# A new front for a long convolution: k without halo rows, a smaller second table, another order

## The chip, the cores and the metric

The kernel runs on one core of a Trainium2 chip. Its time is the device time of one launch in microseconds (us); lower is better. PE, DVE, ACT, POOL and SP are the engines' names in the profile (TensorE, VectorE, ScalarE, GpSimd, SyncE); SP only issues transfers here.

## The reference, cut to what matters

All inputs are bf16; S = 2048 rows, D = 512 channels.

```python
kv = shift(k, 4 taps per channel) * v
y  = causal_convolution(kv, ssm_k) + kv * ssm_D     # FFT of length 2S along S
h  = q + layernorm(q) * y
n  = layernorm(h)
g  = gelu(layernorm(n) @ w1)                          # 512 x 512
x1 = n + shifts_by_quarter(g) @ w2                    # 512 x 512
out = h + x1 + gelu(layernorm(x1) @ w3) @ w4          # 512 x 1792, 1792 x 512
```

## The kernel before, in words

The convolution is done as a Fourier transform in stages on PE. The work, in order:

- *Front.* `load_k`, `load_v`, `load_h` bring k, v and the filter in. `k_transposed` turns rows of k on PE into `kT` (in the slot `kta`). `k_taps` forms the four taps as matmuls of `kT` with `dg`, a row of diagonal matrices with the tap weights (L292), into `psh`; DVE multiplies with v into `kvq` (L404). `k_rows` moves `kvq` into the layout `Rk` by 16 transfers. `h_layout` does the same for the filter on PE (`pt`, evicted into `Rh`). Because rows of k are spread over partitions 16 by 16, the first three rows of a partition need the last rows of the one before it: these are loaded as separate halo rows, with a memset for partition 0 (L270).
- *Tables.* The cosines and sines are made on the chip: POOL writes integers (`iota`, L302), `phase` multiplies them and takes them modulo the circle (L306 on DVE or POOL, L309 on DVE), ACT takes the sine (`sine` L313, `cosine` L318 and L320). The first table is `WA`, the last one `Wf` and its second half `Wf2`. The second table `Wc` is a matrix with zeros except in every fourth column: POOL sets it to zero by 12 memsets (L334), the values are computed in `tta` over 2 x 1024 columns, and four transfers (L354) spread them into `Wc`.
- *First stage* (`stage_a`, L446): 16 tiles for k (`pak`) and 16 for the filter (`pah`), evicted into `Tk` and `Th`.
- *Second stage* (`stage_c`, L470 to L473): products with `Wc`, evicted into `xt`; `product` multiplies the two spectra on DVE (L586, L590, L593) into `Yp`. Between these DVE takes the statistics of q (L552, L553).
- *Back.* `pg` (L647) and its evictions `Gs`, then the last level `py` with `Wf`; `gate` (L711, L713) multiplies with the normalized q (`qn`, L632 and L635) and adds q.
- *MLP.* w1 and w3 by `gelu_mm` (L768), w2 (L828), w4 (L890), with transposes between.

Work is not issued in the order of the program text. Every step is recorded with the steps it depends on, and a list `ISSUE`, written out, gives the order in which all steps are issued and, for a step that two engines can do, the engine (A, V, G). Each engine takes its own steps in that order, and waits where a step is not ready; steps behind it wait too.

```python
for word in ISSUE.split():
    i = int(word.rstrip("AVG"))
    where, fn, deps = self.ops[i][:3]
```

Large buffers lie in named slots that are reused: "C" (k, v, Rk, later Yp), "S1" (filter, later q), "B" (kT, dg, later Tk), "A" (tables, later Th), "W" (Wc, later the weights).

Of the kernel before, what the change touches and what calls it, by code (L numbers as in the profile page):

```python
# [16 lines left out]
P = 128  # L17
S = 2048
# [8 lines left out]
EPS = 1e-5  # L27

# [12 lines left out]
25 3 0 5 7 4 1 2 49 9 26 8 11 29 24 21 6 50V 31 23 13 10 51 16 85 32G 14 22 52 12 20 86V 87 48 15 19 40 74 17 98  # L41
88A 27 34 46 108 35V 99A 37 75 91 109V 53 36 89 39 92 66 76G 28 102 67 90 33 97 100 93 103 62 18 128 30 94 57G
96 47 131 68 101 133 64 38 107 134 132V 104 42 69 105 95 44 63 106 65 77 118 78V 41 79 135V 110 80 54G 83 58 84
45 59 55 112 60 43 119V 129 70 113 71 73 72 111 136 130A 81 117 82 115 122 114 212 137A 120 123 56 61 200 121
138 210 179 201A 208 211V 186 126 209A 127 196 124 187V 197A 206 125 184 116 213 207A 185V 188 214 182 189A 183V
180 139 190 181A 204 202 140G 205V 191A 155 156A 203V 153 163 154A 147 164V 173 148A 174V 151 149 152A 167 141
169 150A 168V 171 170A 177 172V 159 178A 198 160V 175 199A 157 176V 158A 161 192 223 162A 165 239 257 166A 243
194 235 258 195A 261 224 241 193A 259 245 225 142 263 244 260V 265 262A 143 240 237 266A 273 219 144G 264A 275
221 217 277 274A 267 271 276A 289 238 268 272A 287 246 270 278A 283 215 290A 269 285 229 284A 297 280 288A 279
286A 295 236 282 298A 299 281 301 296A 233 313 291 302A 307 292 300A 309 230 294 314A 311 293 308A 242 304 310A  # L50
319 303 312A 321 222 306 325 320A 305 323 231 322A 315 326A 337 316 324A 331 234 317 338A 335 318 332A 333 218
327 345 336A 328 347 334A 343 227 346A 329 349 420 330 348A 385 363 366 226 340 365 344A 339 367 364 228 342
350A 341 145 352 146 351 220 354 353 232 396 216 355 247 356 394 397A 248 358 398 249 357 395A 250 360 359 399A
390 251 400 362 368 391A 252 361 392 253 401V 414 393A 406 254 407V 416 415A 404 417A 255 405V 410 402 411A 408
256 403V 388 409A 386 389V 387A 412 379V 421 413A 380V 371V 373V 370A 418 422 369V 382A 383V 374V 384V 430 378V
423A 372V 375V 381A 424 457 431A 425 428 376A 465 432 458A 426 433 466A 492 429 434 419 500 436 435 427 437 467
377A 438 493A 501A 527 459 441A 468 442A 460 443A 445 469 444A 463 535 446A 470 471 689 464 528A 461 447 472 462
494 448A 473 536A 455 502 477A 495 476A 503 479A 480 496 453 478A 537 481A 449 498 506 454 482 504 456 483A 507
499 451 497 505 538 450 508 486 452 488 487 490 541 512A 484 539 489 511V 491 529 515 485 474 568 530 516A 569
542 531 514A 513V 533 517 532 572 534 540 518A 439 475 543 521 525 440 546A 547V 509 570 522 550 510 571 526 523  # L60
551A 549V 519 548V 575 524 552 520 577 553A 573 595 578 574 579 556 581 554 557 580 576 582 583 558 555 560 559
592 596 585A 584V 561 597 587A 588 594 615 589A 586V 593 565 590 617 618 591A 600 601 544 616 714 562 716 566
715 567 564 692 545 717 563 598 696 693 599 604 690 605 602 698 647 699 697 691 704 649 708 619 705 603 712 606
709 706 713 702 707 607V 700 620 703 608 609V 710 701 648 610 694 711 623 650 627 695 624 613A 718 719 614 653
611V 621 612 625 622 626 628 629 630 651 631 652 659 657 734 658 660 728 671 632 655 735 633 736 654 723 729 738
634 635 672 724 673 674 675 676 636 637 638 645V 639A 643V 646 739 640 737 644 750 725 752 751 677 727 678 742
679 753 680 641V 720 730 642 743 726 748 731 656 722 661 662 732 663 721 685V 749 756 686 744 733 740 687V 745
761 688 754 741 664 746 665 755 666 667 668 788 669 747 670 681V 770 762 771 789 786 763 768 787 799 778 784 779
683V 769 684 757 682 785 764 765 824 758 780 825 759 794 772 781 760 782 773 766 783 774 767 792 775 790 793 776
791 818 777 826 819 804 827 806 805 828 807 820 829 830 821 812 831 800 813 814 801 808 815 822 809 810 816 811  # L70
823 795 817 833 796 832 798 802 803 797 838 834 837 836 835 842 839 841 840 843 844 845
# [3 lines left out]
class Plan:  # L75
# [7 lines left out]
    def __init__(self, rings):  # L83
        self.ops, self.last, self.rd = [], {}, {}
        self.rings, self.tiles = rings, {}

    def add(self, where, fn, r=(), w=(), opens=None, lat=None):
        i = len(self.ops)
        deps = set()
# [32 lines left out]
def kernel(  # L122
# [48 lines left out]
    slot("C", [P, 24064], "kin")  # L171
    slot("S1", [P, DC, S], "hraw")
    slot("B", [P, 11776], "kta")
    slot("A", [P, 16384], "tta")
    slot("W", [P, 3, 16, 4, N2, 4], "Wc")
    slot("S2", [P, N2, 2 * P], "Rh")

    def k_sb():
        return X["kin"][:, 0:9728].rearrange("p (r d) -> p r d", d=D)

    def v_sb():
        return X["kin"][:, 9728:15872].rearrange("p (b t d) -> p b t d", b=3, d=D)

    def Rk():
        return X["kin"][:, 15872:24064].rearrange("p (n d) -> p n d", d=2 * P)

    def kT():
        return X["kta"][:, 0:9728].rearrange("p (c r s) -> p c r s", c=DC, s=P)

    def dg():  # L190
        return X["kta"][:, 9728:11776].rearrange("p (c j s) -> p c j s", c=DC, s=P)

    def trc(a):
        return X["tta"][:, 2048 * a:2048 * a + 2048]

    def uu(i):
        return X["tta"][:, 6144 + 2048 * i:8192 + 2048 * i].bitcast(I32)

    def um():
        return X["tta"][:, 14336:14848].bitcast(I32)  # L200
# [4 lines left out]
    kd = A_k[0]  # L205
    vd = A_v[0].rearrange("(p t) d -> p t d", t=NT)

    def dma(us, fn, r=(), w=()):
        add({"S": us}, fn, r, w)

    def load_k(r0, r1):
        dma(1.4, lambda: nc.sync.dma_start(k_sb()[:, r0:r1, :], bass.AP(
            kd.tensor, kd.offset + (r0 - 3) * D, [[NT * D, P], [D, r1 - r0], [1, D]])),
            r=("C",), w=[("k", r) for r in range(r0, r1)])

    def load_v(qr):
        dma(1.4, lambda: nc.sync.dma_start(v_sb()[:, qr % 3, :, :], vd[:, 4 * qr:4 * qr + 4, :]),
            r=("C",), w=[("v", qr % 3)])

    def load_h(c):  # L220
        dma(1.4, lambda: nc.sync.dma_start(X["hraw"][:, c, :], A_ssm_k[c * P:(c + 1) * P, :]),
            r=("S1",), w=[("h", c)])

    dma(0.5, lambda: nc.sync.dma_start(ssk_bf[:], A_shift_k.rearrange("(c p) j -> p c j", p=P)), w=["sskb"])
    load_k(3, 7)
    for p0, p1 in ((NT, P), (1, NT)):
        dma(0.6, lambda p0=p0, p1=p1: nc.sync.dma_start(k_sb()[p0:p1, 0:3, :], bass.AP(
            kd.tensor, kd.offset + (NT * p0 - 3) * D, [[NT * D, p1 - p0], [D, 3], [1, D]])),
            r=("C",), w=[("kh", p0)])
    load_v(0)  # L230
    load_k(7, 11)
    load_v(1)
    load_k(11, 15)
    dma(0.5, lambda: nc.sync.dma_start(dcol[:], A_ssm_D.rearrange("(c p) -> p c", p=P)), w=["dcol"])
    load_h(0)
    load_h(2)
    load_k(15, 19)
    load_v(2)
    load_h(1)
    load_h(3)  # L240

# [3 lines left out]
    wlo = cst.tile([P, 1], F32)  # L245
    ident = cst.tile([P, P], BF16)
    pidx = cst.tile([P, 1], I32)
    i4 = cst.tile([P, 4], F32)
    pint = cst.tile([P, 6], I32)
# [6 lines left out]
    p64, n2T, k2X, d4X = (pf[:, i:i + 1] for i in (0, 1, 3, 4))  # L256
    k1F, offF = pf[:, 6:7], pf[:, 7:8]
# [4 lines left out]
    def small():  # L262
# [4 lines left out]
        V.memset(wlo[:], -4096.0)  # L267

    add({"V": 0.4}, small, w=["warm", "mpi"])
    add({"V": 0.7}, lambda: V.memset(k_sb()[0:1, 0:3, :], 0.0), r=("C",), w=[("kh", 0)])  # L270
# [9 lines left out]
    def numbers():  # L280
        V.tensor_scalar(pint[:, 0:1], pidx[:], 63, None, op0=OP.bitwise_and)
        V.tensor_scalar(pint[:, 1:2], pidx[:], 2, None, op0=OP.logical_shift_right)
        V.tensor_scalar(pint[:, 2:3], pidx[:], 3, None, op0=OP.bitwise_and)
        V.tensor_scalar(pint[:, 3:4], pidx[:], 31, None, op0=OP.bitwise_and)
        V.tensor_scalar(pint[:, 4:5], pidx[:], 5, None, op0=OP.logical_shift_right)
        V.tensor_scalar(pint[:, 5:6], pidx[:], 6, None, op0=OP.logical_shift_right)
        V.tensor_copy(pf[:, 0:6], pint[:])
# [645 lines left out]
```

## Time and profile before

| what | us |
|---|---|
| three runs | 263.15, 260.5, 263.21 |
| their median | 263.15 |
| span of the profiled execution | 260.4 |
| PE busy | 227.0 (87%) |
| DVE busy | 180.7 (69%) |
| ACT busy | 152.7 (59%) |
| POOL busy | 30.0 (12%) |
| share of DMA engines' time taken by the program's queue | 28.7% |

The profiled execution is told by its span alone, 260.4 us from its first to its last instruction; the lowest of the three times, 260.5, is 0.1 above it. In the first 60 us all engines share the work of the front; from 60 to 110 DVE is busy without a break; from about 127 on PE is. In lines of the timeline the first number is the start in us from the span's beginning, the second the length, and x16 that sixteen like it are drawn together; a bracket tells the idle time before it and what ended it.

### The profile page before, as it was taken

How to read it: one execution, taken by the hardware profiler on the slowest of the kernel's cores; microseconds unless marked ns; L12 is line 12 of the kernel's file. 1: busy time of each engine (PE TensorE's matmuls, PEld its weight loads, DVE VectorE, ACT ScalarE, POOL GpSimd, SP SyncE). 2: the span in 40 equal slices, each digit the busy share in tenths (PEclk: the TensorE clock that was granted, in tenths of full speed). 3: DMA queues.
4: the chain of work that ended last, by engine and by line, in shares of the span. 5: the costliest groups of instructions: out<-in, count | busy, mean ns of one | idle time of the engine just before them, and what ended most of it. 6: DMA issues, size and time to landing. Idle time of an engine off the chain costs nothing.

```text
span 260.4 us, 4761 instructions
## 1 busy us (share of the span) xinstructions
PE 227.0 (87%) x1933; PEld 148.4 (57%) x1946; DVE 180.7 (69%) x410; ACT 152.7 (59%) x194; POOL 30.0 (12%) x37
## 2 busy tenths in 40 slices
PE   2959998989987929657699999999999999999993
PEld 2859998869987918523345454444444444444441
DVE  8895849979999999999999964897290421001341
ACT  2618158997989969999887664524163307604000
POOL 8989200303000000000000000000000000000000
PEclk9986999797999988997799999999999999999999
DMA  6986494970000079200000000020450021000141
GB/s 186 359 320 202 130 256 126 199 149 3 3 1 3 0 269 381 81 0 0 0 3 0 1 0 4 20 60 0 63 123 19 20 63 40 0 0 3 26 95 41
DMA packets 25044, 21.15 MB, mean 81 GB/s; under 512 B 14655, under 2 KB 21823, under 8 KB 24894
## 3 DMA queue, kind: packets, MB, share of 16 engines
q1 hardware_dynamic: 25022, 20.85, 28.7%
q8 instruction: 15, 0.25, 0.4%
q14 instruction: 7, 0.06, 0.1%
HBM read 13.50 MB, written 2.10 MB: 60 GB/s over the span
## 4 chain that ended last, share of the span: by engine, by line
PE 49%; DVE 23%; issue 1%; ACT 1%
PE pw L768 24%; PE p L890 18%; DVE Yp L586 7%; PE p L828 5%; DVE bst L552 3%; DVE Gs L163 2%; DVE Yp L590 2%; DVE Yp L593 2%; PE pt L756 2%; DVE qn L635 1%; DVE wts L711 1%; DVE hh L713 1%; ACT hh L740 1%; DVE mvq L553 1%; DVE xt L163 0%
## 5 line engine op out<-in xcount | busy, mean ns | idle before, releaser
L768 PE MATMUL pw<-act,wts 128*128 128x512 bf16 x285 | 65.3, 383 | 1.5 <-ACT act L161 1.3
L772 ACT ACTIVATE g<-pw 128x512 bf16<-128x512 f32 x56 | 32.5, 596 | 48.9 <-PE pw L768 48.9
L890 PE MATMUL p<-wts,g 128*128 128x512 bf16 x217 | 48.8, 379 | 0.3
L768 PEld LDWEIGHTS <-wts 128*128 128x128 bf16 x288 | 28.4, 99 | 35.4 <-issue 3.1
L895 DVE TENSOR_TENSOR wts<-p,wts 128x1024 bf16<-128x1024 f32 (+1 forms) x9 | 9.9, 1106 | 54.2 <-PE p L890 48.4
L890 PEld LDWEIGHTS <-g 128*128 128x128 bf16 x224 | 21.9, 98 | 26.4
L399 PE MATMUL psh<-kta 128*128 128x128 bf16 x256 | 17.7, 239 | 3.1 <-ACT tta L313 3.1
L586 DVE TENSOR_TENSOR Yp<-xt 128x2048 bf16<-128x2048 bf16 (+1 forms) x20 | 19.3, 999 | 0.0
L399 PEld LDWEIGHTS <-kta 128*128 128x128 bf16 x256 | 17.2, 108 | 3.3 <-issue 3.3
L161 ACT CAST xt<-pch 128x1024 bf16<-128x1024 f32 x16 | 16.1, 1041 | 2.4 <-PE pch L473 1.5
L470 PE MATMUL pck<-Tk,Wc 128*128 128x256 bf16 x64 | 16.1, 290 | 1.6 <-ACT xt L161 1.3
L472 PEld LDWEIGHTS <-Wc 128*128 128x128 bf16 x128 | 14.8, 115 | 2.8 <-issue 2.8
L161 ACT CAST xt<-pck 128x1024 bf16<-128x1024 f32 x15 | 15.2, 1034 | 1.0 <-DVE Yp L586 1.0
L834 DVE SCALAR_TENSOR_TENSOR x<-hh,rho,p 128x512 bf16<-128x512 bf16 x16 | 11.7, 739 | 5.5 <-PE p L828 5.5
L470 PE MATMUL pch<-Th,Wc 128*128 128x256 bf16 x64 | 14.7, 272 | 0.9 <-ACT xt L161 0.7
L473 PEld LDWEIGHTS <-Wc 128*128 128x128 bf16 x128 | 14.8, 115 | 0.5
L828 PE MATMUL p<-wts,act 128*128 128x512 bf16 x61 | 14.8, 379 | 0.2
L404 DVE TENSOR_TENSOR kvq<-psh,kin 128x1024 bf16<-128x1024 f32 x8 | 9.7, 1220 | 7.6 <-PE psh L399 7.6
L470 PEld LDWEIGHTS <-Wc 128*128 128x128 bf16 x128 | 14.8, 115 | 0.1
L473 PE MATMUL pck<-Tk,Wc 128*128 128x128 bf16 x64 | 14.7, 229 | 0.0
L472 PE MATMUL pck<-Tk,Wc 128*128 128x128 bf16 x64 | 14.7, 229 | 0.0
L647 PE MATMUL pg<-CSG,Yp 128*128 128x128 bf16 x128 | 9.3, 236 | 5.8 <-DVE Yp L590 5.1
(130 smaller groups left out, 407.1 us busy)
## 6 DMA issues: line engine op xcount, KB each, us to landing
wts<-in_B_w_dram SPq DMA_DIRECT2D x2, 1792.0 KB, 10.1
kin<-in_A_k_dram SPq DMA_DIRECT2D x4, 512.0 KB, 7.1
kin<-in_A_v_dram SPq DMA_DIRECT2D x4, 512.0 KB, 6.9
hraw<-in_A_ssm_k_dram SPq DMA_DIRECT2D x4, 512.0 KB, 9.0
kin<-kvq SPq DMA_DIRECT2D x16, 128.0 KB, 3.3
q_sb<-in_A_q_dram SPq DMA_DIRECT2D x2, 1024.0 KB, 10.6
out_dram<-wts SPq DMA_DIRECT2D x14, 128.0 KB, 2.3
Wc<-tta SPq DMA_DIRECT2D x4, 384.0 KB, 5.6
```

The costliest lines, as they stand in the source:

```text
L161: A.copy(o, src)
L399: T_.matmul(pv[:, i, c * P:(c + 1) * P], lhsT=kT()[:, c, t0 + i + 3 - j, :], rhs=dg()[:, c, j, :], start=(j == 0), stop=(j == 3))
L470: T_.matmul(pv[:, kk, :, :].rearrange("p r d -> p (r d)"), lhsT=W[0], rhs=Tw.rearrange("p r d -> p (r d)"), start=True, stop=False)
L472: T_.matmul(pv[:, kk, 0, :], lhsT=W[1], rhs=Tw[:, 1, :], start=False, stop=False)
L473: T_.matmul(pv[:, kk, 1, :], lhsT=W[2], rhs=Tw[:, 0, :], start=False, stop=True)
L586: v(0.08 + 1.14 * s, lambda i=i: V.tensor_tensor(out=pr(i), in0=x(0), in1=x(1)[:, i:i + 1].to_broadcast([P, 2, n, 8]), op=MUL), ["C"] + rx ...
L768: T_.matmul(ps[:], lhsT=wt(w)[:, k, m * P:(m + 1) * P], rhs=xT()[:, k, 4 * b * P:(4 * b + 4) * P], start=(k == 0), stop=(k == DC - 1))
L772: add({"A": 0.59}, lambda: A.activation(dst(), X[pkey][:], ACT.Gelu_apprx_tanh), r + [pkey, "gelu"], [key])
L828: T_.matmul(ps[:, i, :], lhsT=gT()[:, m, t + i + 2 + off[m], :], rhs=wt("w2")[:, m, :], start=(m == 0), stop=(m == 3))
L834: v(0.74, lambda t=t, i=i, key=key: V.scalar_tensor_tensor(out=X["x1"][:, t + i, :], in0=hn()[:, t + i, :], scalar=rho[:, t + i:t + i + 1] ...
L890: T_.matmul(ps[:, i, :], lhsT=X["g2"][:, b % 2, m, s0:s0 + P], rhs=wt("w4")[:, m, :], start=(m == 0), stop=(m == FC - 1))
L895: v(0.62 * (hi - lo), lambda j=j, lo=lo, hi=hi, key=key: V.tensor_tensor(out=obb()[:, j, lo:hi], in0=X[key][:, lo:hi], in1=ofb()[:, j, lo: ...
```

## The change

- k is loaded first, in four quarters; v has four buffers instead of three, so that its last quarter needs no buffer to come free. The halo rows, their transfers, their transposes and the memset go: `kT` has two more columns per row, and a tap that reaches back into the row before reads `kT` one column further left. The quarters of k are then needed together: a quarter's taps need its own transposes and those of the quarter before it (for the first, the last).
- The second table is computed over 512 columns instead of 2 x 1024, in the slot of `kT`, and 16 transfers instead of four spread it, each a quarter of a partition set; `Wc` has another layout.
- The filter lies in one slot with the integers of the last table ("A"), and q has a slot of its own from the start.
- `Wf2` is copied with a sign from `Wf` (four copies of 64 partitions), not computed.
- 32 matmuls on zeros stand ahead of PE's first transposes.
- The statistics of q are put together by six operations on all 16 tiles at once, not by an aggregate for each tile.
- `ISSUE` is new throughout, and with it engines: DVE takes 15 of the 32 evictions of the first stage (12 before) and 3 of the 16 of `Gs` (5 before).

The core of the diff (the list of numbers left out):

```diff
-    slot("S1", [P, DC, S], "hraw")
-    slot("B", [P, 11776], "kta")
-    slot("A", [P, 16384], "tta")
-    slot("W", [P, 3, 16, 4, N2, 4], "Wc")
+    slot("S1", [P, NT, D], "q_sb")
+    slot("B", [P, 16384], "kta")
+    slot("A", [P, 16384], "hta")
+    slot("W", [P, 3, 4, 4, N2, 16], "Wc")
...
+        V.memset(zero[:], 0.0)
...
-    for hf in range(2):
-        iota(1.15, lambda hf=hf: uu(hf), [[16, 8], [256, 32], [4, 4]], 1 + 128 * hf, ("u", hf))
-        phase(0.75, lambda hf=hf: uu(hf), n2T, 0.0, ("u", hf))
+    iota(0.6, uw, [[256, 32], [4, 16]], 1, "uW", ["B"])
+    phase(0.4, uw, k2X, kq64, "uW", ["B"], True)
+    sine(0.5, lambda: trc()[:, 1], uw, "uW", ("t", 1), False, ["B"])
+    add({"V": 0.2}, lambda: V.tensor_scalar(trc()[:, 2], trc()[:, 1], -1.0, None, op0=MUL),
+        ["B", ("t", 1)], [("t", 2)])
+    cosine(0.5, lambda: trc()[:, 0], uw, "uW", ("t", 0), ["B"])
...
-    for d in range(4):
-        dma(1.5, lambda d=d: nc.sync.dma_start(
-            X["Wc"][d:P:4, :, :, d].rearrange("p a b c d -> p (a b) (c d)"),
-            X["tta"][d:P:4, 0:6144].rearrange("p (a x) -> p a x", a=48)),
+    for kq in range(4):
+        for d in range(4):
+            dma(0.62, lambda d=d, kq=kq: nc.sync.dma_start(
+                X["Wc"][d:P:4, :, kq, d].rearrange("p a c d -> p a (c d)"), trc()[N2 * kq:N2 * kq + N2]),
+                r=["B", "W"] + [("t", a) for a in range(3)] + [("wz", kq, j) for j in range(3)],
+                w=[("Wc", d, kq)], x=(0.6, 2.1))
...
+        def row(c, t):
+            return kT()[:, c, t, 2:KP] if t >= 0 else kT()[:, c, t + NT, 1:KP - 1]
...
-                        T_.matmul(pv[:, i, c * P:(c + 1) * P], lhsT=kT()[:, c, t0 + i + 3 - j, :],
+                        T_.matmul(pv[:, i, c * P:(c + 1) * P], lhsT=row(c, t0 + i - j),
                                   rhs=dg()[:, c, j, :], start=(j == 0), stop=(j == 3))
...
+    warm_up(32)
+    k_transposed(3)
+    for qr in range(4):
+        if qr < 3:
+            k_transposed(qr)
...
+            def turned(e, hf=hf, c=c):
+                (V if e == "V" else G).tensor_scalar(
+                    Wf2[N1 * c:N1 * c + N1, 16 * hf:16 * hf + 16, :],
+                    Wf[N1 - N1 * c:P - N1 * c, 0, 16 * hf:16 * hf + 16, :], 1.0 if c == hf else -1.0, None, op0=MUL)
```

What the new list makes of the engines' orders at the start: POOL has the small iotas, the identity, 2 memsets of `Wc`, 2 iotas of 1024, 2 memsets, one step of 1024, then 8 memsets in a row. DVE has the numbers, the steps of all small integer tables, the masks (`mk`), the negated sine, then `dg`, two evictions of `kT`, three steps of `CSG`, three steps of 1024 integers, and then the first product of `psh` with v. PE has the zeros, three quarters of transposes of k, the taps of the second quarter, the last transposes, then taps and filter transposes in turn, all 16 filter tiles of the first stage, then those of k. SP has k, the tap weights, k, v, two quarters of the filter, the first transfer into `Wc`, the other two quarters, then the transfers of `Rk`, `Wc` and v mixed, q after the last of them, and the weights.

More of the change, by code (lines that the diff above doesn't have):

```diff
@@ L211, in load_k, with dma @@
[L211 to L214, printed above, removed]
+    def dma(us, fn, r=(), w=(), x=(1.55, 2.2)):
+        add({"S": us}, fn, r, w, x=x)
+    def load_k(qr):
+        dma(0.43, lambda: nc.sync.dma_start(k_sb()[:, 4 * qr:4 * qr + 4, :], kd[:, 4 * qr:4 * qr + 4, :]),
+            r=("C",), w=[("k", qr)])
@@ L225 @@
[L225 to L229, printed above, removed]
+        dma(0.5, lambda: nc.sync.dma_start(hraw()[:, c, :], A_ssm_k[c * P:(c + 1) * P, :]),
+            r=("A",), w=[("h", c)])
+    load_k(3)
+    dma(0.45, lambda: nc.sync.dma_start(ssk_bf[:], A_shift_k.rearrange("(c p) j -> p c j", p=P)), w=["sskb"], x=(0.3, 2.2))
@@ L243 @@
+    for h in range(2):
+        dma(0.6, lambda h=h: nc.sync.dma_start(X["q_sb"][h * N1:(h + 1) * N1, :, :], qd[h]), r=["S1"], w=[("q", h)], x=(5.4, 2.2))
     warm = cst.tile([P, 1], F32)
@@ L267, in small @@
         V.memset(wlo[:], -4096.0)
-    add({"V": 0.4}, small, w=["warm", "mpi"])
-    add({"V": 0.7}, lambda: V.memset(k_sb()[0:1, 0:3, :], 0.0), r=("C",), w=[("kh", 0)])
+        V.memset(zero[:], 0.0)
+    add({"V": 0.5}, small, w=["warm", "mpi", "zero"])
+    add({"V": 0.1}, lambda: V.memset(kT()[:, :, 13:NT, 0:2], 0.0), r=("B",), w=["kz"])
     add({"A": 1.5}, lambda: A.activation(warm[:], warm[:], ACT.Sin), r=["warm"], w=["sin"])
@@ L346 @@
[L346 to L358 removed]
+            slotkey + ["mpi", "sin", key], [okey])
@@ L367, with warm_up, pe, k_transposed @@
                                            mk[:, d:d + 1], None, op0=MUL), ["mk", "sc"], [("CSG", d)])
-    def k_transposed(r0, r1):
-        key = ("pk", r0)
+    def warm_up(n):
+        key = ("pz", n)
+        def pe():
+            pz = psum("psa", key)
+            for i in range(n):
+                T_.matmul(pz[:, 0:P], lhsT=zero[:, 0:P], rhs=zero[:, 0:P], start=True, stop=True)
+        add(mm(n), pe, ["zero"], [key], opens=("psa", key))
+    def k_transposed(qr):
+        key = ("pk", qr)
         def pe():
```

327 lines of the change are left out of this document (154 added, 173 removed), and 4 rows, old and new, of the table ISSUE.

## The prediction

> **What bounds the kernel now.** I read the page first, then the chain that ended last in order of time, then the timelines of PE, DVE and POOL from the start of the span, since the edits lie there.
>
> ```profile
> span 260.4 us, 4761 instructions
> PEclk9986999797999988997799999999999999999999
> PE 49%; DVE 23%; issue 1%; ACT 1%
> ```
>
> The slowest two thirds of the chain are PE (the MLP), its first third is DVE. The four stations of the DVE part, in the chain and in DVE's timeline:
>
> ```profile
> 58.97 2.47 DVE L552 BATCH_NORM_STATS2 bst<-q_sb 128x6 f32<-128x512 bf16 x4 [2.12 <-DMA q_sb<-in_A_q_dram]
> ...
> 101.04 1.13 DVE Gs L163
> ...
> 110.51 0.61 DVE wts L711
> ```
>
> From 58.97 to 110.5 DVE never stops: statistics of q (L552), the complex products (L586, L590, L593), Gs evictions, qn, then the first gate (L711). From about 127 PE runs without a hole to the end. Before 58.97 the order is PE's:
>
> ```profile
> 11.56 3.73 PE L399 MATMUL psh<-kta 128*128 128x128 bf16 x64
> 18.43 6.50 PE L399 MATMUL psh<-kta 128*128 128x128 bf16 x64 [3.13 <-ACT tta L313]
> ...
> 36.87 3.75 PE L399 MATMUL psh<-kta 128*128 128x128 bf16 x64
> 40.55 2.31 PE L446 MATMUL pah<-WA,Rh 64*128 64x128 bf16 x40
> ```
>
> The tap matmuls (psh) start at 11.56, PE pauses 3.1 us, comes back at a low clock (64 matmuls in 6.50 instead of 3.73), and stage_a starts at 40.55. I call that moment X. What I think decides this case is in DVE's and POOL's timelines:
>
> ```profile
> 8.48 0.98 DVE L359 TENSOR_SCALAR mk<-i,pf 128x4 f32<-128x4 f32 x1
> 9.22 2.29 DVE L292 TENSOR_TENSOR kta<-ident,ssk_bf 128x2048 bf16<-128x2048 bf16 x1
> 12.56 2.29 DVE L306 TENSOR_SCALAR tta<-tta,pf 128x1024 int32<-128x1024 int32 x1 [1.05 <-POOL tta L302]
> ...
> 30.32 0.69 DVE L309 TENSOR_SCALAR tta<-tta 128x1024 int32<-128x1024 int32 x1
> ```
>
> ```profile
> 7.60 1.83 POOL L334 MEMSET Wc<- 128x1024 uint32 x2
> 9.40 3.12 POOL L302 IOTA tta<- 128x1024 int32 x1
> 12.47 1.83 POOL L334 MEMSET Wc<- 128x1024 uint32 x2
> 14.27 1.52 POOL L302 IOTA tta<- 128x1024 int32 x1
> ...
> 20.76 3.62 POOL L334 MEMSET Wc<- 128x1024 uint32 x4
> ```
>
> A TENSOR_SCALAR of DVE from SBUF to SBUF takes 0.69 for 1024 columns when POOL is idle, and 2.29 when it meets POOL's memsets: begun at 12.56, it ends at 14.85, 0.55 after the second memset has ended (14.30). One of four columns takes 0.98, to the end of the memset at 9.43. So such an operation waits for POOL, and a pair of memsets was not interrupted for it. PSUM evictions (L404, 1.2 us each) do not care.
>
> **The change part by part.** The sum of before is X 40.55, then 18.4 to the first statistics, 42.1 to the last product (101.04), 9.4 to the first gate, and 150.0 to the end: 260.4. The times given are 263.15, 260.5 and 263.21; this execution is one like 260.5.
>
> *Tables and order, up to X.* The second table shrinks from 2x1024 to 512 columns; of the Wc memsets all 12 stay, but in a new order: 2, two iotas, 2, one TENSOR_SCALAR, then 8 in a row. On DVE the diagonal dg (L292 before), which every tap matmul needs, now stands behind the whole work on the small tables: 11 SBUF TENSOR_SCALARs and one more for the negated sine. In before dg started at 9.22 because the shift weights landed at 9.1; they are now issued second and should land near 5.4, which alone would let PE start 2 to 3 us earlier. But POOL's list, by its rows, is: ident ready 2.4, 2 memsets of 0.91, 2 iotas of 1.03, 2 memsets, one TENSOR_SCALAR of 1.2, with about 1 us of DVE's turns in between, so the run of 8 starts at 10.4 and ends at 10.4 + 8 x 0.905 = 17.6. DVE gets about one turn at each change of POOL's operation: five or six turns before 10.4, which serve the conversion of the partition numbers, both steps of uA, uW, uH and the second of uW. The steps of uG, mk and the negated sine are then caught by the run. After 17.6: these five 1.2, dg 2.3, two evictions of kT at 1.15 each: 23.4 for the first psh instead of 11.56.
>
> From there PE is the limit: 64 psh for 5.1 (between 3.73 and 6.50, since PE has stood idle; both ends kept), 16 transposes 1.07, six groups of 32 psh at 1.87, four groups of h transposes at 1.9: 19.9. X = 23.4 + 5.1 + 19.9 = 48.4. Without any waiting for POOL dg would run from 5.5 to 9, psh would start at 11.2, and X would be 35.5 to 38. These are the two ends.
>
> *Halo rows, warm-up.* Twelve transposes, one ACT copy (1.44) and two transfers go; 32 matmuls on zeros come, 32 x 0.058 to 32 x 0.118 = 1.9 to 3.8 us from about 1 to 5. They end before the first k lands (5.11). Zero either way; they can raise the clock early, but PE then waits again.
>
> *16 transfers for 4, k, v, h, q loads.* Each issue costs SP 0.6 (the rows of L412 and L354), so 16 instead of 4 add 7 us of SP time, spread between the Rk transfers. h0 and h1 stand behind the first of them, which needs three memsets of the run or before it; h is wanted by PE only after 27, so nothing. q is issued behind the last Rk and Wc, about X + 5; its second half took 13.0 from issue to landing, so X + 18: DVE is free for it at X + 18.8. That cover is 0.8 us thin; past it, each microsecond late counts fully.
>
> *stage_a.* DVE takes 15 of 32 evictions (12 before) and ACT 17 (20 before); DVE loses one 0.69 step of the filter. DVE's last ends at X + 1.4 + 15 x 1.16 = X + 18.8, against 18.4: +0.4.
>
> *The filter's second half.* Two iotas, four steps and two sines go (ACT 2 x 1.17 in the middle, DVE 2 x 0.65), four half-width POOL copies come. Nothing shows a 64x1024 bf16 copy on POOL; between 0.4 (L350 on DVE) and 1.3 (POOL's 1024 int32). Nobody waits for it before the last level, 40 us later: zero.
>
> *Statistics and products.* Of 16 statistics 11 stand before the last product: 11 x 0.60 = 6.6. Products: six full at 3.6, four half at 1.87: 29.1. No aggregates (16 x 0.09), no xt eviction (1.1). 35.7 instead of 42.1: -6.4. ACT has all 32 xt at 0.93 = 29.8 beside DVE's 29.1; as a bound +0.7, taken as 0.
>
> *End of products to gate.* Five statistics 3.0, 15 dependent small operations at 0.20 (the pitch of L532 to L537) 3.0, two qn 0.6, three Gs 3.4, six qn 1.9: 11.9 to 12.0, against 9.4: +2.6. Gs goes to ACT 13 times at 0.93 = 12.1 and runs beside it from 4 us before.
>
> *The rest.* The same PE work in another order: 150.0, with 2 us either way.
>
> Sum: X + 18.8 + 35.7 + 12.0 + 150.0 = X + 216.5, so the break-even is X = 43.9. With X = 48.4 it is 264.9; I write 265, against the profiled 260.4; against the median it is less, and I leave it there.
>
> **The rivals.**
> *No waiting that matters* (12%): POOL and DVE pass each other and X = 37: 253.5. For it: L350 and many steps after 28 show no delay. Against: L306, L359, L360 were all delayed when POOL worked.
> *The port changes hands at each memset* (32%, not slower): DVE gets a turn every 0.95 us also inside the run. Then dg starts near 13.6, psh at 18.1, and the first kvq product ends at 22.6, behind three CSG and three filter steps; PE has 18.8 left: X = 41.4, 258. For it: iotas let DVE in at 9.43, 14.30 and 15.79. Against: 12.56. The Trainium skill, "SBUF — State Buffer", section "SBUF: two separate sides", speaks for this one: the shared pair of ports goes to the operation that starts first and for one whole instruction, and a two-input operation contends only with a GpSimd operation that reads. By that, a step begun at 12.56 should have gone before the memset of 13.36, and the trace does not show it.
> *Between these* (10%): the run holds, but the small steps slip in before it; X = 43 to 44: 260.5.
> *Slower still* (6%): q or the xt evictions set the pace as well: 2 us late q, 2 us of ACT: 269.
>
> **How the numbers follow.** Forecast 40%: 265, its own range 262 to 268. About 1% (2.6 us) is what a measurement of this kernel can tell from no change. Faster: all of the first rival and half of the second with a little of the third, 0.30; same: the other half, most of the third and the forecast's edge, 0.22; slower: 0.48. Range: 253 to 269.
>
> **What would show it.** On POOL eight memsets in a row from about 10 to 18; on DVE a TENSOR_SCALAR of 17 columns or mk with several us; dg starting near 19; PE's first psh near 23 and X near 48; statistics at X + 19. If dg starts before 12 and psh at 14 or less, the forecast is wrong at its first step and the time is under 258. If the statistics wait for q, the thin cover is gone. If X is as said and the time is not X + 216.5, the later terms are wrong.

## The result, and the profile after

The changed kernel takes 270.61 us (median; 269.38 to 272.83) against 261.82 for the kernel before: a ratio of 1.035, 95% interval 1.027 to 1.043. Ratios, here and below, leave out executions that took over 1.5% more than the fastest of their kernel; medians and ranges are of all. The profiled execution has a span of 267.6 us, 7.2 more than the 260.4 of before. "Slower" was the likeliest outcome given, but 265 and the upper end of the range, 269, were both too low.

From the page of the changed kernel, the span, the granted clock in 40 slices, and the shares of the chain that ended last:

```profile
span 267.6 us, 4805 instructions
PEclk9689999779999979598699999999999999999999
PE 48%; DVE 33%; SPq 8%; DMA 5%; issue 3%; ACT 2%; DVEq 0%
```

SPq (SP's issuing) and DMA hold 13% of this line. The line of the kernel before cannot be set against that, because its chain could be followed back only to 63.3 us; there, too, the first statistics waited 2.12 us for q, which landed at 58.88, 18.3 behind X. The chain in order of time, by some of its pieces (start, length, what):

```profile
50.63 12.35 DMA q_sb<-in_A_q_dram
...
100.37 2.99 DVE bst L568 x5
106.18 0.73 DVE qn L652 x2
106.91 1.14 DVE Gs L169
...
113.68 0.70 DVE wts L728
```

The chain goes through the load of q, which was to be hidden, then through DVE's statistics and products to the first gate at 113.68. The rows of DVE, PE and POOL that answer to those of before:

```profile
7.92 0.92 DVE L346 TENSOR_SCALAR kta<-kta 128x512 bf16<-128x512 bf16 x1
8.75 2.27 DVE L303 TENSOR_TENSOR kta<-ident,ssk_bf 128x2048 bf16<-128x2048 bf16 x1
63.07 1.29 DVE L568 BATCH_NORM_STATS2 bst<-q_sb 128x6 f32<-128x512 bf16 x2 [1.00 <-DMA q_sb<-in_A_q_dram]
```

```profile
13.87 3.13 PE L420 MATMUL psh<-kta 128*128 128x128 bf16 x36
18.74 1.74 PE L420 MATMUL psh<-kta 128*128 128x128 bf16 x28 [1.74 <-ACT kta L167]
...
41.19 1.31 PE L466 MATMUL pah<-WA,Rh 64*128 64x128 bf16 x24
```

```profile
2.45 2.16 POOL L351 MEMSET Wc<- 128x1024 uint32 x2
...
6.78 1.90 POOL L351 MEMSET Wc<- 128x1024 uint32 x2
8.68 3.33 POOL L320 TENSOR_SCALAR hta<-hta,pf 128x1024 int32<-128x1024 int32 x1
11.96 1.83 POOL L351 MEMSET Wc<- 128x1024 uint32 x2
17.67 5.42 POOL L351 MEMSET Wc<- 128x1024 uint32 x6 [3.88 <-DMA Wc<-kta]
```

The diagonals (L303) start at 8.75 and not at 19; the run of eight memsets never was one, because POOL waited 3.9 us for the first transfer into Wc. So X is 41.2, hardly later than before's 40.55, and the time was lost behind it (all in us):

| stretch | before | after | forecast |
|---|---|---|---|
| start to X (first stage_a matmul) | 40.55 | 41.2 | 48.4 |
| X to first q statistics | 18.4 | 21.9 | 18.8 |
| to last product | 42.1 | 37.3 | 35.7 |
| to first gate | 9.4 | 13.3 | 12.0 |
| first gate to the end of the last rsqrt chain | 29.5 | 33.5 | 150.0, with the next row |
| that to the end | 120.4 | 120.4 | in the row above |

The rsqrt chains are the small dependent steps (L544 to L549) that make the reciprocal square roots of the layer norms; "the gates" below means the stretch of the fifth row.

### The profile page after: what moved, and what is told of

Read it like the earlier page. It is cut to its first block, busy times and chain, and to the rows that moved or that the text cites. A ratio compares the mean times of both kernels' runs of the same rounds, so it can differ in the third digit from the quotient of the medians.

```text
span 267.6 us, 4805 instructions
## 1 busy us (share of the span) xinstructions
PE 231.7 (87%) x1966; PEld 151.2 (57%) x1966; DVE 179.8 (67%) x387; ACT 150.9 (56%) x198; POOL 29.9 (11%) x33
## 4 chain that ended last, share of the span: by engine, by line
PE 48%; DVE 33%; SPq 8%; DMA 5%; issue 3%; ACT 2%; DVEq 0%
PE pw L785 20%; PE p L907 18%; DVE Yp L603 7%; DMA q_sb<-in_A_q_dram 5%; SPq L356 4%; DVE bst L564 4%; PE p L845 4%; SPq L432 4%; PE psh L420 3%; DVE bst L568 3%; DVE Yp L610 2%; DVE hh L730 2%; DVE Yp L607 2%; DVE wts L728 2%; PE pk L399 1%
## 5 line engine op out<-in xcount | busy, mean ns | idle before, releaser
L785 PEld LDWEIGHTS <-wts 128*128 128x128 bf16 x288 | 28.4, 99 | 36.8 <-issue 4.8
L491 PEld LDWEIGHTS <-Wc 128*128 128x128 bf16 x128 | 19.4, 151 | 0.2 <-issue 0.2
L493 PEld LDWEIGHTS <-Wc 128*128 128x128 bf16 x128 | 19.2, 150 | 0.0
L420 PE MATMUL psh<-kta 128*128 128x128 bf16 x256 | 16.3, 226 | 3.1 <-ACT kta L167 1.7
L664 PE MATMUL pg<-CSG,Yp 128*128 128x128 bf16 x128 | 10.7, 249 | 9.0 <-DVE Yp L610 4.9
L494 PEld LDWEIGHTS <-Wc 128*128 128x128 bf16 x128 | 18.3, 143 | 0.0
L420 PEld LDWEIGHTS <-kta 128*128 128x128 bf16 x256 | 15.4, 102 | 3.5 <-ACT kta L167 1.9
L167 ACT CAST xt<-pck 128x1024 bf16<-128x1024 f32 x16 | 16.1, 1029 | 0.9 <-PE pck L494 0.9
L491 PE MATMUL pch<-Th,Wc 128*128 128x256 bf16 x64 | 16.0, 284 | 0.0
L167 ACT CAST Gs<-pg 128x1024 bf16<-128x1024 f32 x13 | 12.1, 1069 | 6.7 <-PE pg L664 6.7
L664 PEld LDWEIGHTS <-Yp 128*128 128x128 bf16 x128 | 9.4, 114 | 10.2 <-DVE Yp L610 5.0
L494 PE MATMUL pch<-Th,Wc 128*128 128x128 bf16 x64 | 14.6, 228 | 0.0
L494 PE MATMUL pck<-Tk,Wc 128*128 128x128 bf16 x64 | 14.5, 227 | 0.0
```

Source lines behind the costliest of these rows:

```text
L167: A.copy(o, src)
L420: T_.matmul(pv[:, i, c * P:(c + 1) * P], lhsT=row(c, t0 + i - j), rhs=dg()[:, c, j, :], start=(j == 0), stop=(j == 3))
L491: T_.matmul(pv[:, kk, :, :].rearrange("p r d -> p (r d)"), lhsT=W[0], rhs=Tw.rearrange("p r d -> p (r d)"), start=True, stop=False)
L493: T_.matmul(pv[:, kk, 0, :], lhsT=W[1], rhs=Tw[:, 1, :], start=False, stop=False)
L494: T_.matmul(pv[:, kk, 1, :], lhsT=W[2], rhs=Tw[:, 0, :], start=False, stop=True)
L664: T_.matmul(pv[:, ee, :], lhsT=X["Yp"][:, (8 * i + ee) * P:(8 * i + ee + 1) * P], rhs=CSG[:], start=True, stop=True)
```

## The experiments

Three theories on the loss: *A*, the new order behind the first gate puts dependent DVE steps back to back (4 us). *B*, the 16 transfers into Wc on SP's one queue make the last quarter of Rk and q late (3 us). *P*, POOL's port goes over to DVE at the end of each memset. A fourth, *L*, comes with experiment 7. The rivals stand in the expectations. The ratios of the changed kernel's variants in experiments 1, 3 and 5 to 7 lie between 1.013 and 1.021, with intervals of up to 0.01 either way, and cannot be told from one another; what is said of their parts rests on one profiled execution each. Line numbers in the experiments are mostly two lower than in the changed kernel, since the written order is shorter.

**1. The old order behind the swap of the PSUM pools.** The code of these steps (over 400) is the same in both kernels, so their order and engines can be exchanged. VectorE's first ones, for illustration:

```diff
-410V 411V 412V 413V 414V 415V 418V 419V 420V 422V 423V 421V 424V
+410V 411V 414V 418V 412V 419V 415V 420V 422V 421V 413V 423V 453V 424V
```

> The changed kernel up to the swap of the PSUM pools, and every step behind it in the order (and on the engines) that the kernel before has; the code of these steps is the same in both. Theory A (the loss behind the first gate is the new order, which puts VectorE steps that need one another back to back): from the first gate to the end of the last rsqrt chain of the gates 33.4 us falls to about 29.4, all ahead of it stays (first gate near 113.7), the span goes from 267.6 to about 263.6. Rival (the low PE clock at 125 to 132 us, or what the front left behind, stretches the gates): the stretch stays at about 33 and the span at about 267.6.

Measured: gates 113.66 to 143.20, 29.5 us; span 264.7; ratio to the kernel before 1.016 (1.008 to 1.024). DVE's timeline from the first gate, changed kernel first, then the old order:

```profile
113.68 0.69 DVE L728 TENSOR_TENSOR wts<-wts,qn 128x1024 bf16<-128x1024 bf16 x1 [1.37 <-ACT wts L167]
114.41 0.69 DVE L730 TENSOR_TENSOR hh<-wts,q_sb 128x1024 bf16<-128x1024 bf16 x1
115.13 0.69 DVE L564 BATCH_NORM_STATS2 bst<-hh 128x6 f32<-128x512 bf16 x1
115.86 0.18 DVE L565 BATCH_NORM_AGGREGATE mvh<-bst 128x2 f32<-128x6 f32 x1
115.96 0.66 DVE L564 BATCH_NORM_STATS2 bst<-hh 128x6 f32<-128x512 bf16 x1
```

```profile
115.72 0.67 DVE L726 TENSOR_TENSOR wts<-wts,qn 128x1024 bf16<-128x1024 bf16 x1
116.31 0.69 DVE L562 BATCH_NORM_STATS2 bst<-hh 128x6 f32<-128x512 bf16 x1
116.92 0.67 DVE L728 TENSOR_TENSOR hh<-wts,q_sb 128x1024 bf16<-128x1024 bf16 x1
117.51 0.17 DVE L563 BATCH_NORM_AGGREGATE mvh<-bst 128x2 f32<-128x6 f32 x1
```

Look at starts, not lengths. A step that needs its predecessor starts 0.03 to 0.04 after that one's end (113.68 + 0.69, next 114.41); one that does not starts 0.08 before it (115.72 + 0.67, next 116.31). Only the first of the rows shown has a wait, both orders look "busy" throughout, and the difference is 0.12 us for every such pair. In the old order 38 of the gates' 96 steps behind the first start after their predecessor's end, in the new one 67 of 95. Summed over the gates, the overlap less the gaps is 3.4 us in the old order and nothing in the new one, and DVE's work there is 0.7 longer in the new one: together the 4.0. PE's granted clock is no rival: it was 0.50 for 12 us of this run's gates, and 0.57 to 0.89 for 12 us of before's, and the two stretches are of one length, 29.54 and 29.55. Only 2.9 of the 4.0 reach the end, because the stretch behind grew by 1.1; whether PE's low clock did this was not tried apart.

**2. The mirror.** The kernel before, with the changed kernel's order behind the swap.

> The mirror: the kernel before up to the swap of the PSUM pools, and every step behind it in the order and on the engines of the changed kernel. Theory A: from the first gate to the end of the last rsqrt chain of the gates 29.4 us grows to about 33.4, the span from 260.4 to about 264.4. Rival (the order is not the cause, the state in which the front leaves the chip is): the stretch stays near 29.4 and the span near 260.4.

Measured: gates 108.57 to 142.13, 33.6 us; ratio 1.011 (1.007 to 1.014). Theory A holds both ways: all profiles with the old order here have 29.5 to 29.6 us in this stretch, all with the new one 33.5 to 33.6. The span is 262.3, not 264.4, because X fell to 38.1 in this execution with an unchanged front. Between 18 and 25 us PE's granted clock was 1.00 here and 0.55 in the first profile of the kernel before. So X of one front differs by 2.4 us between executions, and the 40.55 on which the forecast built was a late one.

**3. The old order from the products on, statistics of q among them.**

> As the run with the old tail, and the products, the q statistics, the first square-root chain, the Gs evictions and qn too in the order and on the engines of the kernel before (the 16 aggregates stay away, the longer chain is spread between the same neighbours). Theory A: besides the 4.0 of the gates, the stretch from the first q statistics to the first gate, 50.6 us in the changed kernel, falls by what the chain and the late statistics cost it, about 2: some 48.5; span near 261.6. Rival (these steps cost VectorE the same wherever they stand, so only what its busy time says): the stretch stays at 50 to 51 and the span comes out as with the old tail alone.

Measured: from the first statistics (62.03) to the first gate (113.57) 51.5 us, no less than the 50.6 in the changed kernel; span 264.8, ratio 1.020 (1.010 to 1.030). The rival is right for this part: with the statistics early, the last product ends later (103.7 instead of 100.4) and the gate follows sooner.

**4. q early, and the last quarter of Rk ahead of six Wc transfers, all on SP.** SP's steps alone (18 is the last load of the filter, 20 and 21 are q, 128 to 131 Rk's last quarter, 54 to 66 transfers into Wc):

```diff
-18 111 ... 54 66 61 57 64 128 65 129 130 131 63 59 20 21
+18 20 21 111 ... 54 66 128 129 130 131 61 57 64 65 63 59
```

> The changed kernel, only SP's order is other: the two loads of q right behind the loads of the filter (near 17 us, where SP waits), and the four transfers of the last quarter of Rk ahead of the last six transfers into Wc. Theory B (16 transfers at 0.65 us in one queue make Rk's last quarter and q late): VectorE's waits of 1.14 and 0.69 us at Tk and of 1.00 us for q go, the first q statistics move from 63.07 to about 60.3 and the span from 267.6 to about 264.8. Rival (the transfers themselves are slow because the DMA engines are busy, or the evictions set the pace anyway): q still lands after 60 or the first statistics stay within 0.7 us of 63.07.

Measured: worse, span 271.9, ratio 1.040 (1.032 to 1.048); X 46.8. DVE's waits up to 68 us:

```profile
DVE kvq L422 <- DMA Wc<-kta: 6.7, 1, 6.7
DVE kvq L422 <- PE psh L418: 6.4, 5, 2.5
```

The releaser named is not the whole of it. The product of the third quarter (39.48) overwrites rows that the transfers of Rk's first quarter read; the last of those landed at 39.36, against 33.94 in the changed kernel, and the third quarter of v at 37.2 against 26.7. Both were issued behind q, whose halves landed at 28.4 and 34.6. On SP's queue the transfers of this run all landed in the order of their issue, and the two loads of 1 MB moved those issued behind them back: the next seven took 9.3 to 15.2 us to land, and 2.5 to 4.3 in the changed kernel. This run did not test theory B, it moved the loss.

**5. Fifteen of the Wc transfers on ScalarE's queue; and only four made at all.** Both with the old order behind the swap.

```diff
-nc.sync.dma_start(X["Wc"]...
+(nc.sync if (d, kq) == (1, 1) else nc.scalar).dma_start(X["Wc"]...
```

> The kernel with the old tail (span 264.7), and 15 of the 16 transfers into Wc issued by ScalarE's queue behind its two sines of the filter (ScalarE waits from 20.8 to 33.8 us there); the order on SP is otherwise kept. Theory B (Rk's last quarter and q are late because SP issues 15 more transfers ahead of them, 0.65 us each, and lands them in order): Rk's last quarter is issued at once when its rows are ready, near 42.5 to 45, q right behind, the first q statistics move from 63.15 to about 60.3 and the span to about 261.9. Rival (the DMA engines are the limit, or ScalarE's issuing delays its evictions by as much): the first statistics stay after 62.5, or X grows by what is gained.

> The kernel with the old tail, and only four of the 16 transfers into Wc are made (those of the second quarter of k1); the other twelve are left out, with three quarters of the second table left at zero. It prices the twelve transfers on SP's queue with nothing put in their place. Theory B: first q statistics near 60.3, span near 261.9, as with the transfers on the other queue. Rival (stage_a's evictions and the order of its two halves set the 21.9 us from X to the first statistics): they stay near 63, span near 264.7.

Measured: X to first statistics 19.5 us (61.45 less 41.98) and 20.5 (62.41 less 41.95), against 22.0 in the run with the old tail; spans 262.8 and 263.8; ratios 1.014 (1.005 to 1.022) and 1.015 (1.007 to 1.022). SP's own timeline, changed kernel and then the run with the other queue:

```profile
45.27 0.62 SPq L432 DMA_DIRECT2D kin<-kvq  x1
45.94 0.61 SPq L356 DMA_DIRECT2D Wc<-kta  x1
46.60 1.97 SPq L432 DMA_DIRECT2D kin<-kvq  x3
48.62 1.32 SPq L356 DMA_DIRECT2D Wc<-kta  x2
49.98 1.25 SPq L251 DMA_DIRECT2D q_sb<-in_A_q_dram  x2
```

```profile
43.33 2.95 SPq L430 DMA_DIRECT2D kin<-kvq  x4
46.33 1.26 SPq L249 DMA_DIRECT2D q_sb<-in_A_q_dram  x2
```

Rk's last quarter and q go out 2 to 4 us earlier once the Wc transfers are elsewhere, and DVE no longer waits for q. Theory B holds from X on, with 2.6 us by the one run and 1.6 by the other, where 2.8 was expected; what held the second back was not tried. In all, seven profiles with the sixteen transfers on SP in this mixed order have 21.9 to 22.2 us in this stretch, and six with eight or fifteen of them on ScalarE's queue 19.2 to 20.7. The first statistics themselves came at 61.45 and 62.41, not at the 60.3 expected, since X was 0.9 later in both. Of that, 0.8 is the first group of tap matmuls, 3.84 us instead of 3.04 in the run with the old tail, at a granted clock of 0.50 and 0.57; it is no cost of the other queue, as the run with four transfers has it too.

**6. The memsets as one run, out of the small steps' way.** Old tail; the twelve memsets behind POOL's iotas and its step of the filter; then this with experiment 5's queue.

> The kernel with the old tail, and GpSimd's twelve memsets of Wc moved behind its iotas and its one step of the filter, so that they come as one run from about 6 us on; the first transfer into Wc goes behind the loads of the filter. Theory P (the port changes hands at each memset's end, so that a small VectorE step pays about 1 us beside memsets): the steps ahead of the diagonals meet few memsets, the diagonals start at 6 to 7.5 instead of 8.75, the first tap matmul at 11.5 to 12.5 instead of 13.9, X falls from 41.1 to about 39, the span to about 262.5. My forecast's rule (a run of memsets is not interrupted): what VectorE has left at 6 us waits for the run's end near 17, the first tap matmul comes near 21, X near 47 and the span above 270.

> All three together: old tail, transfers into Wc on ScalarE's queue, memsets behind. If the parts add: 264.7 less 2.8 less 2.1, near 259.8, about the kernel before (260.4). If the front's gain is lost because the rows of k wait for loads (rival), it comes out like the run with the other queue alone, near 261.9.

Measured: POOL and, beside it, DVE:

```profile
6.12 12.76 POOL L349 MEMSET Wc<- 128x1024 uint32 x12
```

```profile
6.33 0.81 DVE L368 TENSOR_SCALAR mk<-i,pf 128x4 f32<-128x4 f32 x1
7.18 0.86 DVE L369 TENSOR_SCALAR mk<-mk 128x4 f32<-128x4 f32 x1
7.26 0.92 DVE L344 TENSOR_SCALAR kta<-kta 128x512 bf16<-128x512 bf16 x1
8.10 2.27 DVE L301 TENSOR_TENSOR kta<-ident,ssk_bf 128x2048 bf16<-128x2048 bf16 x1
```

This is the unbroken run that my forecast feared, and DVE's steps get into it at the ends of the memsets (7.10 and 8.02 here), two of them at each, at 0.8 to 0.9 us each, whatever their size. The diagonals (two inputs) take their usual 2.27 beside two memsets. The Trainium skill's "SBUF — State Buffer", section "SBUF: two separate sides", says just this of operations with two SBUF inputs; the trace agrees. The forecast's rule does not hold here, but the gain of theory P was mis-sized: the tap matmuls began only 0.65 earlier, and X did not move (41.3). Spans 265.9 and 265.1, ratios 1.016 (1.007 to 1.026) and 1.013 (1.006 to 1.021): the parts do not add. In both runs DVE now waits 2.0 and 2.3 us for xt from ACT, so ScalarE held the products back there.

**7. Another layout of the transposed k.** One line; first alone in the changed kernel, then with 1 and 5.

```diff
-rearrange("p (c r s) -> p c r s", c=DC, s=KP)
+rearrange("p (r c s) -> p c r s", c=DC, s=KP)
```

> The changed kernel in its own order, with one line other: the transposed k lies by rows and then by column blocks, not by blocks and then by rows, so that the four rows of one eviction lie together. Theory L (an eviction into kta waits for tap matmuls of other rows, and they for it, because their stretches of the tile overlap when the blocks come first): ScalarE's eviction of the last quarter no longer waits 8.1 us for the tap matmuls, PE's waits of 1.7 and 1.3 us for kta go, X falls from 41.2 to about 38. Theory B on top of it (SP's queue runs without a gap and lands q last): the first q statistics stay near 62 to 63 all the same, since q is issued no earlier than some 49 us, and the span falls by 1 at most. Rival to L (these waits are true ones, on the psum ring or on DMA): X stays within 0.7 of 41.2. Rival to B: the first statistics fall with X to about 60, the span to 264.5.

> Old tail, transfers into Wc on ScalarE's queue, and the other layout of the transposed k. Theory L and B together: X near 38.5 instead of 42.0, and here the first statistics fall with it, from 61.5 to about 58, the span from 262.8 to 259 to 260. Rival (ScalarE with its 32 xt evictions is by now the limit of the products): part of it comes back as VectorE's wait for xt, 2 us or more in the stretch from the first statistics to the first gate, and the span stays at 261 or above.

Measured, first alone. Of PE's and ACT's waits from 13 to 45 us in the changed kernel, those at kta, in that order:

```profile
PE psh L420 <- ACT kta L167: 1.7, 1, 1.7
PE psh L420 <- DVE kta L169: 1.3, 1, 1.3
```

```profile
ACT kta L167 <- PE psh L420: 8.1, 1, 8.1
```

With the new layout none of the three is in the table of waits, and from the first tap matmul to X it takes 23.7 us instead of 27.3. Theory L holds: evictions and matmuls waited for each other over rows they do not share. The second profile of the changed kernel in experiment 9 makes the fair pair: its tap matmuls began at the same 16.8, the mean granted clock was 0.97 in both, and with the old layout it took 27.2. X itself was 40.5 and not 38, which by itself was the rival's sign, because the tap matmuls began 2.9 late (experiment 9). The first statistics came at 62.63, as q landed at 62.54: theory B, once more. Ratio 1.021 (1.017 to 1.025).
With the transfers on ScalarE the tap matmuls ended at 37.8 instead of 42.0, but X was 40.7: PE waited 2.9 us for the eviction of Rh, which stood on ScalarE behind the transfers. Span 261.3, ratio 1.017 (1.010 to 1.025).

**8. The best of these, and the layout in the kernel before.** Old tail, the layout, eight transfers on ScalarE and eight on SP.

> The best that the experiments point to: the changed kernel with the old tail, the other layout of the transposed k, and the eight transfers into Wc of the third and fourth quarter issued by ScalarE behind the sines of the filter, the other eight left on SP. If theories A, B and L hold and ScalarE is free again before its eviction of the filter near 34 us: X near 38, q issued near 42, first q statistics near 57, first gate near 108, end of the last rsqrt chain 29.5 later, span 258 to 259.5, a little below the kernel before (260.4). Rival (the two queues fight for the same DMA engines, or ScalarE's xt evictions now set the products): first statistics near 59 or the stretch to the first gate 52 and more; span 260.5 to 262.

> The kernel before with the other layout of the transposed k alone. Theory L, if it holds there too: PE's wait of 3.1 us in front of the second quarter's tap matmuls goes, X falls from 40.55 by up to 3 and, as q is issued behind stage_a there and has no SP backlog, the first statistics and the span fall nearly as much: 257.5 to 259.5. Rival (that wait is the late table work of ScalarE, which evicts the next quarter only behind its sines): X and the span stay within 0.7 of 40.55 and 260.4.

Measured: X 38.6, first statistics 57.8, first gate 108.4, span 259.6; ratio 1.004 (0.9998 to 1.007). Some 3% are recovered and the kernel before is reached, not beaten. In the kernel before the layout brings nothing that can be told from its own scatter (X 39.5, and its wait of 3.4 us for ScalarE's sines stays; ratio 1.004, 1.001 to 1.007): the rival holds.

**9. The race.** Experiment 7's first run had its diagonals at 11.67, with the changed kernel's own order in front. So the changed kernel was profiled in two more executions, the best kernel in one, and in a fourth run the memsets were taken out of the way altogether.

> The changed kernel as it is, looked at in one more execution. Theory R: either the diagonals start at 8.75 and the time is near 269.4 as in the first look, or they start near 11.7 and the time is 272 or more. Rival: the diagonals start at 8.75 whatever the time is.

> The same kernel in a third execution, with the same two outcomes: diagonals at 8.75 and some 269 us, or at 11.7 and 272 or more (theory R); or diagonals at 8.75 beside a time of 271 and more (rival).

> The best kernel so far in one more execution; its times lay between 260.8 and 268.0. Theory R: 261 to 262 with the diagonals at 8.75, or 264 and more with the diagonals near 11.7. Rival: no such pairing.

> The best kernel so far (span 259.6, median 263.65), and all twelve memsets of Wc behind GpSimd's two additions into the filter, which wait for its loads (some 18 to 20 us), so that no VectorE step on the small tables ever meets a memset; GpSimd's two iotas and one step of the filter stay where they are. The transfers into Wc go behind Rk's first two quarters. Theory R (a race: a waiting VectorE step gets its turn between two memsets in most executions, 8.75 for the diagonals, and in others only behind both, 11.67 as in the run with the layout alone; what is lost there delays all that follows): the diagonals start near 6.8 in every execution, X near 37, the span near 258, and the times scatter as little as those of the kernel before: median 259.5 to 261, no run above 265. Rival (the scatter of 261 to 268 comes from the granted clock or from DMA): the diagonals start earlier all the same, but the times still scatter to 266 and more, and the median stays at 262 to 264.

Measured: changed kernel 268.63 us with diagonals at 8.76 (X 40.6), and 271.14 with diagonals at 11.67 (X 44.0). POOL and DVE in the second:

```profile
2.46 1.84 POOL L351 MEMSET Wc<- 128x1024 uint32 x2
...
9.77 1.83 POOL L351 MEMSET Wc<- 128x1024 uint32 x2
```

```profile
2.37 1.98 DVE L323 TENSOR_SCALAR kta<-kta 128x64 int32<-128x64 int32 x1
2.48 2.13 DVE L318 TENSOR_SCALAR kta<-kta,pf 128x512 int32<-128x512 int32 x1
...
8.81 2.94 DVE L346 TENSOR_SCALAR kta<-kta 128x512 bf16<-128x512 bf16 x1
11.67 2.27 DVE L303 TENSOR_TENSOR kta<-ident,ssk_bf 128x2048 bf16<-128x2048 bf16 x1
```

The two steps that took 0.20 and 1.25 in the first profile take 1.98 and 2.13 here, past the end of the second memset (4.30). So both outcomes occur in one program, worth 2.9 us at the diagonals and about 3 in X: a race. Of twelve profiles with this pair of memsets ahead of the small steps, ten have the diagonals at 8.75 or 8.76 and two at 11.67; nothing here tells what decides it. It doesn't explain all of the scatter. The best kernel took 263.75 with diagonals at 8.75, where I expected 262 at most. Without memsets ahead of them (diagonals at 6.86, tap matmuls from 11.99 to 35.5) the times still went from 260.3 to 267.9, with a median of 264.9 against 262.5 for the kernel before; its ratio is 0.999 (0.994 to 1.003). Its profile is of an execution of 266.51 us. X was 41.5 there, 6.0 behind the tap matmuls, since ScalarE held its eviction of Rh back behind transfers that waited for the memsets.

**10. Eight transfers on GpSimd's queue,** with the memsets as in 9: behind its first copy of the filter's second half, then ahead of it.

> As the run with the memsets behind the filter's additions, but ScalarE issues nothing: the eight late transfers into Wc go on GpSimd's own queue behind its memsets (GpSimd has nothing else until 44 us), and SP issues Rk's third quarter ahead of its own eight. Theory Q (in the run before, X was late because ScalarE stood at the head of its queue with transfers that waited for the memsets to end at 31.3, ahead of its eviction of the filter): without that, X comes right behind the tap matmuls, near 35.7 instead of 41.5, the first q statistics near 55 to 57 (q's landing decides), the first gate near 107, and the span near 257 to 258. Rival (the transfers on GpSimd's queue come so late or so slowly that the evictions into Tk, which overwrite their source, wait for them; or ScalarE becomes the bound of the products): the first statistics stay at 58 or more, the span at 259.5 or more.

> As the run before it (X 36.2, but VectorE and ScalarE then waited 8.6 us for transfers into Wc that GpSimd issued only at 40.2 to 44.9, behind its first copy of the filter's second half, and that landed behind q), with one change: GpSimd's eight transfers stand right behind its memsets, ahead of that copy. Theory Q: they are issued from 32.3 on and landed by 41, nothing waits at Tk, X stays near 36, the first q statistics come near 56 to 57 with q's landing, the first gate near 107, span 257 to 258.5, median below that of the kernel before. Rival (GpSimd's transfers are slow to issue or to land whatever their place): a wait at Tk of 2 us or more stays, first statistics at 59 or later, span 260 or more.

Measured: X 36.2 and 36.9, near the 35.7 and 36 expected, so ScalarE's queue was what held it. In the first run the copy came ahead of the transfers, which were issued at 40 to 45; VectorE and ScalarE waited 8.6 and 8.7 us at Tk, which overwrites their source, and the ratio is 1.031 (1.026 to 1.036). In the second they were issued at 33.2 and that wait is gone; span 261.2, ratio 1.001 (0.998 to 1.005). But the first statistics came at 59.5, 22.6 behind X and 1.2 after q had landed. PE had stage_c's first matmuls (from 52.4) between the last of stage_a, and its matmuls of 256 columns took 0.42 us there and 0.28 from 58 on (granted clock 0.64 and 1.00). Whether that is the cause was not tried. No version here beats the kernel before by more than its measurement can tell.

## Why the prediction was wrong

- **X, the main step: wrong.** The forecast let a run of memsets hold back the last small steps, and with them the diagonals, to 17.6, so that the tap matmuls began at 23.4. They began at 13.87, since the small steps got in at the ends of the memsets, and in a real run of twelve (6) they did so too. The rule was read from one row of before, the step at 12.56 that waited through two memsets. That row is no accident: it took 2.29 us in all three profiles with before's front. But it was one case, and other steps did not do as it did; what sets them apart is open.
- **From the tap matmuls to X: 25.0 forecast, 27.3 measured.** The evictions into kT and the tap matmuls waited for each other, which no term of the sum had; with the other layout (7) it was 23.7. So X was 48.4 less 9.5 and plus 2.3. The second rival, priced at X = 41.4, had the place right and the size by luck: its tap matmuls begin at 18.1, 4.2 too late, and it has 23.3 from there. Its sum, 258, failed with the later terms, and so did the forecast's sign that diagonals before 12 and tap matmuls by 14 mean a time under 258. A small slip beside these: without any waiting, its own terms give X = 34.8 to 37.6, not 35.5 to 38.
- **SP and q: the cover was seen, the cost was not.** I had 7 us of issues and a cover of 0.8, and put the issues "spread between the Rk transfers", q at X + 5. q was issued at X + 8.8 and landed at X + 21.8, and Rk's last quarter waited behind Wc transfers as well. The stretch is 3.1 longer than forecast; experiment 5 gives 1.6 to 2.6 of it to the transfers.
- **Statistics, products, to the gate: 47.7 forecast, 50.6 measured.** The steps taken away were priced by their own time. DVE's work in this stretch fell by 7.1 us, from 59.2 to 52.1, but its overlap less the gaps fell too, from 7.7 to 2.9, and the first gate waited 1.4 for ScalarE, so that only 0.9 of the 7.1 was won. Full products stayed at 3.8 us instead of my 3.6, and half products took 2.1 instead of 1.87. Which of the steps that were moved or taken away had carried the overlap was not tried apart; the old order without the aggregates (3) did not shorten the stretch.
- **The rest, 150.0 with 2 either way: 153.9.** "The same PE work in another order" overlooked that the first 30 us of it are DVE's, whose new order costs 4.0. This is shown both ways, by 1 and 2.
- Halo rows, warm-up, filter's second half: nothing in the trace speaks against their zeros; none was tried alone. POOL's four copies took 2.8 us each, not the 0.4 to 1.3 bounded, but nobody waited for them in the changed kernel.

That the forecast came as near as it did was luck: an error of 7.2 in X, too late, stood against 9.9 us, too short, in the four later stretches.

## What to carry to other kernels

An order of DVE's steps is worth microseconds that no wait shows: put between two dependent steps one that needs neither, and price a removed small step by what its neighbours then do. Before splitting one transfer into many, count what is queued behind them on that engine, and ask when the last one is issued, not how long one lasts. A single delayed row is a case, not a rule: before a forecast hangs on it, look for the other rows of the same kind. And a total that comes out near does not bear out its terms: compare each stretch with its own.

## What was not expected of the hardware

- A VectorE step of 4 columns beside GpSimd's memsets took as long as one of 512 (0.81 and 0.92 us), against 0.22 without memsets (experiment 9), and the same program had its diagonals 2.9 us earlier or later from execution to execution.
- Beside the diagonals (2.27 us both times), GpSimd's step of 1024 columns took 3.33 us, and 1.47 when they were not running (experiment 6): there VectorE won.
- A load of 1 MB into 64 partitions (a half of q) landed 7.6 to 9.0 us after its issue, and the second one 12.2 to 13.4 after its own, in all profiles but those of experiment 4 and the first of experiment 10.
